# Attention and two expert layers on one core: a narrow key layout for seven pairs of heads, and a fourth tile for the parts of the weights

## The chip, the cores and the metric

The kernel runs on one core of a Trainium2 chip. The metric is the device time in microseconds of one execution, the median of the runs. TensorE (PE, with its weight loads as PEld), VectorE (DVE), ScalarE (ACT) and GpSimd (POOL) are the engines; nearly all transfers are issued from SyncE's queue (SP) and run on the core's 16 DMA engines.

## The reference

Attention over 4 batches of 8 heads, 576 positions of 64 values, with rotary positions on q and k; then a dense layer (512 to 2048 to 512, leaky), then a layer of 8 experts (512 to 1024 to 512) of which each token takes the best one. All in float32.

```python
q_rot, k_rot = rotate(q), rotate(k)
scores = scale * q_rot @ k_rot.T
attn = exp(scores - max); attn = attn / (sum(attn) + 1e-9)
x = (attn @ v)                        # 2304 tokens x 512
h = x @ w_in; x = maximum(0.01 * h, h) @ w_out
out[mask] = gate * relu(x[mask] @ w1[e]) @ w2[e]   # for each expert e
```

## The kernel before

Float32 precision is kept by splitting values into two f16 (or fp32r) parts, a high and a low one, and adding up the products of the parts. Attention works on 16 pairs of heads (g = 0 to 15) and 9 units of each (128 queries of one head; the ninth unit holds the last 64 queries of both heads), 144 units in all.

One pass of `step(i)` (L1006) is written out by hand. It emits the exponential of unit i-1 (L519), the row maximum of unit i (L514), the high and the low part of the weights of unit i-1 into a tile `P` (L525 on ScalarE, L531 on VectorE), its transposition by DMA into `PT` (L535), the product with v of unit i-4 (`LAG` = 4, L552), its evacuation (L562), and the scores of unit i+1 (L507). The order of these letters stands in `ORDER1` (before the dense layer runs), `ORDER2` and `ORDER3`. `P` has 3 buffers, `PT` has 4. Between them, by a budget for each engine, run jobs: the preparation of the next pair, the decoding of the dense layer's weights (`weights`, L201, until about 250 us), and the work on finished rows. After the rows of the first blocks are done, each step also takes one unit of the dense layer: twelve products into `h` (L266), leaky (L274, L278), a split (L282, L286) and six products into `acc` (L297).

`prep(g)` (L372) rotates q and k of a pair, scales them and splits them. The parts go to a staging tile `stg` of four blocks: q's parts of head 0, q's parts of head 1, the high parts of the keys of both heads, and the low ones (`stacks`, L410; `hi`, L417, on ScalarE; `lo`, L423, on VectorE). One DMA transposition makes `kt` from the two key blocks (L472), and in a later piece another makes `stk[:, 0:2]` from the two q blocks (L476). Four copies from `kt` then fill `stk[:, 2:6]` (L479), so that each head has its high keys twice, on partitions 0 to 63 and 64 to 127, and its low keys twice. The scores of a unit are then two products for each half of the keys, with 128 rows each: both parts of q by the high keys, and both parts of q by the low keys. After the copies, the load of the next pair's q and k is issued (L370). `stg` has one buffer, `stk` two.

Of the kernel before, what the change touches and what calls it, by code (L numbers as in the profile page):

```python
# [11 lines left out]
F16 = mybir.dt.float16  # L12
# [9 lines left out]
B, H, S, D = 4, 8, 576, 64  # L22
# [30 lines left out]
NMERGED = 60  # L53
ADDG = 0
HI_A1 = 1
TICK2 = 3
RATE1 = dict(A=2, V=1.8, G=1.4)
RATE2 = dict(A=2, V=2.1, G=1.6)
# [32 lines left out]
def _pow2(nc, pool, sq2, n, inv):  # L91

    t = pool.tile([128, n], U32, name="pt", tag=f"pt{n}")
    s = pool.tile([128, n], F32, name="ps", tag=f"ps{n}")
    nc.vector.tensor_scalar(out=t, in0=sq2.bitcast(U32), scalar1=0xFFFFFFFF, scalar2=24, op0=ALU.bitwise_xor, op1=ALU.logical_shift_right)
    nc.vector.tensor_scalar(out=s.bitcast(U32), in0=t, scalar1=-50.0, scalar2=2.0 ** 23, op0=ALU.add, op1=ALU.mult)
    nc.vector.tensor_scalar(out=inv.bitcast(U32), in0=t, scalar1=-2.0 ** 23, scalar2=304.0 * 2 ** 23, op0=ALU.mult, op1=ALU.add)
    return s
# [3 lines left out]
def attention_moe_kernel(ctx: ExitStack, tc: tile.TileContext, qkv, w_in, w_out, emb, tau, w1, w2,  # L102
                         rope, ident, tokc, iota, pcol, out):
    nc = tc.nc
# [28 lines left out]
    def ps_h():  # L133
        return psH.tile([128, 512], F32, name="h")
# [51 lines left out]
    def decode(raw):  # L186

        hw, lw = raw[:, :, 1], raw[:, :, 0]
        yield Piece(A=1.2, tick=M.tick + (TICK2 if M.unit else TICK))
        nc.scalar.activation(out=hw.bitcast(F32), in_=hw.bitcast(F32), func=AF.Copy, scale=2.0 ** -112)  # L190
# [160 lines left out]
    at = ExitStack()  # L351
    qkp = at.enter_context(tc.tile_pool(name="qkp", bufs=1))
    stp = at.enter_context(tc.tile_pool(name="stp", bufs=2))
    pep = at.enter_context(tc.tile_pool(name="pep", bufs=2))
# [17 lines left out]
    def prep(g):  # L372
        i0 = 9 * (g - 1)
        v16 = v16s[g % 2]
        raw, rawv = raws.pop((g, 2)), raws.pop((g, 1))[:, 0]
        sq = small.tile([128, 3], F32, name="sq3")
        cs, sn = tab[:, 0], tab[:, 1]
        if g:
            t2 = qkp.tile([128, 2, 2, 5, 64], F32, name="t2", tag="stg")
            t2 = [t2[:, t] for t in range(2)]  # L380
        else:
            t2 = [mp.tile([128, 2, 5, 64], F32, name=f"t2{t}", tag="xT", bufs=XTB) for t in range(2)]

        def square(t):
            nc.scalar.activation(out=junk, in_=(raw[:, t] if t < 2 else rawv).rearrange("p h c d -> p (h c d)"), func=AF.Square, accum_out=sq[:, t:t + 1])

        def rope_s(t, eng=nc.gpsimd):
            for z in range(2):
                o, i = 32 * z, 32 - 32 * z
                eng.tensor_tensor(out=t2[t][:, :, :, o:o + 32], in0=raw[:, t, :, :, i:i + 32],  # L390
                                        in1=sn[:, :, o:o + 32].unsqueeze(1).to_broadcast([128, 2, 5, 32]), op=ALU.mult)

        def rope_c(t):
            xf = raw[:, t].rearrange("p h c d -> p h (c d)")
            nc.vector.tensor_tensor(out=xf, in0=xf, in1=cs.rearrange("p c d -> p (c d)").unsqueeze(1).to_broadcast([128, 2, 320]), op=ALU.mult)

        def add(t, eng=nc.vector):
            eng.tensor_tensor(out=raw[:, t], in0=raw[:, t], in1=t2[t], op=ALU.add)

        m3 = small.tile([128, 3], F32, name="m3")  # L400
        sc = small.tile([128, 2], F32, name="sc")

        def scales(pb):
            s3 = _pow2(nc, small, pb[:, 0:3], 3, m3)
            nc.vector.scalar_tensor_tensor(out=sc[:, 0:1], in0=m3[:, 0:1], scalar=0.125, in1=m3[:, 1:2], op0=ALU.mult, op1=ALU.mult)
            nc.vector.tensor_scalar(out=sc[:, 1:2], in0=sc[:, 0:1], scalar1=-1.0, scalar2=None, op0=ALU.mult)
            return s3


        def stacks():  # L410
            stg = qkp.tile([128, 4, 5, 128], F16, name="stg")
            s2 = stg.rearrange("p s c x -> p (s c x)")
            qhi = s2[:, 0:1408].rearrange("p (h x) -> p h x", h=2)[:, :, 0:640].rearrange("p h (c x) -> p h c x", c=5)[:, :, :, 0:64]
            return (s2, qhi, stg[:, 2].rearrange("p c (h x) -> p h c x", h=2), [stg[:, 0, :, 64:128], stg[:, 1, :, 0:64]],
                    [stg[:, 3, :, 64 * h:64 * h + 64] for h in range(2)])

        def hi(out, t):  # L417
            if g and (HIQ, HIK)[t]:
                nc.vector.tensor_scalar(out=out, in0=raw[:, t], scalar1=s3[:, t:t + 1], scalar2=None, op0=ALU.mult)
            else:  # L420
                nc.scalar.activation(out=out, in_=raw[:, t], func=AF.Copy, scale=s3[:, t:t + 1])

        def lo(out, t, high):  # L423
            for h in range(2):
                nc.vector.scalar_tensor_tensor(out=out[h], in0=raw[:, t, h], scalar=s3[:, t:t + 1], in1=high[:, h], op0=ALU.mult, op1=ALU.subtract)

        if g == 0:
            rope_s(1)
            rope_s(0, nc.vector)
            for t in range(3):  # L430
                square(t)
            rope_c(0)
            add(0)
            pb = ps_h()
            nc.tensor.matmul(pb[:, 0:3], lhsT=ones, rhs=sq, start=True, stop=True)
            s3 = scales(pb)
            s2, qhi, khi, qlo, klo = stacks()
            hi(qhi, 0)
            rope_c(1)
            add(1)  # L440
            hi(khi, 1)
            lo(klo, 1, khi)
            lo(qlo, 0, qhi)
        else:
            yield Piece(A=0.72, G=1.64, at=max(i0 - EARLY, 0), tick=M.loaded + TLOAD)
            square(0)
            rope_s(0)
            yield Piece(A=0.72, V=0.74, G=1.64)
            square(1)
            rope_c(0)  # L450
            rope_s(1)
            yield Piece(A=0.72, V=0.74)
            square(2)
            add(0, nc.gpsimd if g < ADDG else nc.vector)
            yield Piece(V=0.74)
            rope_c(1)
            yield Piece(G=1.5)
            add(1, nc.gpsimd)
            pb = yield from total(sq, 3)
            yield Piece(must=True, V=0.35)  # L460
            s3 = scales(pb)
            s2, qhi, khi, qlo, klo = stacks()
            yield Piece(A=1.44)
            hi(qhi, 0)
            hi(khi, 1)
            yield Piece(V=0.93)
            lo(klo, 1, khi)
            yield Piece(V=0.93)
            lo(qlo, 0, qhi)
        yield Piece(at=i0 - 2)  # L470
        kt = stp.tile([128, 2, 640], F16, name="kt", bufs=1)
        nc.sync.dma_start_transpose(out=kt.rearrange("p s (c x) -> p (s c) x", c=5), in_=s2[:, 1280:2560])  # L472
        yield Piece(at=i0 - 1)

        stk = stp.tile([128, 6, 640], F16, name="stk")
        nc.sync.dma_start_transpose(out=stk[:, 0:2].rearrange("p s (c x) -> p (s c) x", c=5), in_=s2[:, 0:1280])  # L476
        for h in range(2):
            for z in range(2):
                nc.sync.dma_start(out=stk[64 * z:64 * z + 64, 2 + 2 * h:4 + 2 * h], in_=kt[64 * h:64 * h + 64])  # L479
        pairs[g] = (stk, s3, sc, v16)  # L480
        if g + 1 < 4 * B:
            load(g + 1, 2)
        vjobs.append(Job(prep_v(g, v16, rawv, s3)))
# [15 lines left out]
    def a_scores(g, u):  # L499
        stk = pairs[g][0]  # L500
        ps = psS.tile([128, 2, 512], F32, name="S")
        todo = [(u % 2, u // 2 * 128, 128, 0)] if u < 8 else [(0, 512, 64, 0), (1, 512, 64, 64)]
        for n in range(2):
            ks = slice(288 * n, 288 * n + 288)
            for h, c0, m, o in todo:
                for a in range(2):
                    nc.tensor.matmul(ps[o:o + m, n, 0:288], lhsT=stk[:, h, c0:c0 + m], rhs=stk[:, 2 + 2 * h + a, ks], start=(a == 0), stop=(a == 1))  # L507
        return ps

    def a_max(g, u, ps):  # L510
# [9 lines left out]
        return e  # L520

    def a_hi(e, i):
        p = pep.tile([128, 2 * S], F16, name="P", bufs=3)
        if i % (HI_ACT if M.unit else HI_A1) == 0:
            nc.scalar.activation(out=p[:, 0:576], in_=e, func=AF.Copy, scale=P_UP)  # L525
        else:
            nc.vector.tensor_scalar(out=p[:, 0:576], in0=e, scalar1=P_UP, scalar2=None, op0=ALU.mult)
        return p
# [440 lines left out]
    n = len(units)  # L969
# [227 lines left out]
    g = gates(0, NCH)  # L1197
# [10 lines left out]
    x = e_xt(3)  # L1208
# [92 lines left out]
```

## Time and profile before

| | us |
|---|---|
| median of 3 runs | 1064.49 |
| lowest and highest | 1061.05, 1064.89 |
| the profiled execution | 1062.26 |
| its span | 1060.5 |
| attention, first to last exponential | 29 to 663 |
| dense layer, first to last product of L266 | 182 to 794 |
| experts | about 800 to 1060 |

All times below are microseconds from the start of the span, in one profiled execution. An engine's busy time leaves out waits; a wait is named by the instruction that waited and by what came last of what it waited for. A row of the timeline gives start, length, engine, line, operation, output and inputs, the count of instructions merged into it, and in brackets the idle time before it with its releaser. The granted clock is 1.00 at TensorE's full 2.4 GHz and 0.50 at 1.2 GHz.

### The profile page before, as it was taken

Reading aid. Unit: us, or ns where it says so; the run is one execution under the profiler, and the core shown is the slowest. Engines: PE = TensorE matmul, PEld = TensorE weight load, DVE = VectorE, ACT = ScalarE, POOL = GpSimd, SP = SyncE. Lnnn points to the kernel's source line nnn. Section 1 sums busy time; section 2 is a strip of 40 time slices with the busy share of each in tenths; the row PEclk is TensorE's granted clock in tenths of the full one; section 3 lists DMA queues with packets and bytes.
Section 4 is the critical chain, followed back from the end, with each engine's and each line's share of the span. In section 5 each row is a group of like instructions: output and inputs, shape, how many; then the busy total and the mean of one; then the engine's idle time right before and its main releaser. Section 6 shows DMA issues by size and latency. Waiting matters only on the chain. (4 is left out here: it accounts for less than half of the span.)

```text
span 1060.5 us, 19876 instructions
## 1 busy us (share of the span) xinstructions
PE 882.0 (83%) x6737; PEld 709.4 (67%) x6737; DVE 773.9 (73%) x1564; ACT 755.8 (71%) x1439; POOL 360.6 (34%) x414
## 2 busy tenths in 40 slices
PE   1455454777888899989898899999999899999997
PEld 1344243565666787767677677778877778888885
DVE  6988798778867874767768766313476999999893
ACT  6987687777767774877777677535345888888883
POOL 1333323252443452544444533322233361211111
PEclk9995555989989999999999999999999999999999
DMA  7899889788487694696795784301152111115190
GB/s 227 192 219 243 194 165 214 171 178 196 91 163 159 120 180 98 122 177 125 140 198 126 125 162 91 66 1 41 31 180 101 40 61 40 51 50 199 34 334 33
DMA packets 269005, 141.41 MB, mean 133 GB/s; under 512 B 236248, under 2 KB 244696, under 8 KB 268897
## 3 DMA queue, kind: packets, MB, share of 16 engines
q1 hardware_dynamic: 265696, 130.11, 54.9%
q0 software_dynamic: 3200, 9.97, 2.9%
q8 instruction: 55, 0.90, 0.4%
q14 instruction: 54, 0.43, 0.1%
HBM read 120.04 MB, written 10.49 MB: 123 GB/s over the span
## 5 line engine op out<-in xcount | busy, mean ns | idle before, releaser
L266 PE MATMUL h<-xT,wi 128*128 128x256 f16 (+1 forms) x1920 | 218.2, 265 | 36.9 <-DVE g L278 31.2
L266 PEld LDWEIGHTS <-wi 128*128 128x128 f16 x1920 | 170.6, 100 | 83.5 <-issue 63.8
L286 POOL TENSOR_TENSOR gl<-g,gh 128x256 fp32r<-128x256 f32 x144 | 110.7, 769 | 317.2 <-ACT gh L282 293.5
L297 PE MATMUL acc<-wo,gh 128*128 128x512 f32 x576 | 196.6, 423 | 0.0
L531 DVE SCALAR_TENSOR_TENSOR P<-E,P 128x576 f16<-128x576 f32 x144 | 127.6, 886 | 92.7 <-ACT P L525 91.8
L552 PE MATMUL o<-v,PT 128*128 128x65 f16 (+3 forms) x1770 | 104.1, 216 | 66.3 <-DMA PT<-P 46.0
L552 PEld LDWEIGHTS <-PT 128*128 128x128 f16 (+1 forms) x1770 | 92.5, 112 | 85.2 <-DMA PT<-P 58.9
L507 PE MATMUL S<-stk 128*128 128x288 f16 (+1 forms) x640 | 115.4, 332 | 36.4 <-ACT E L519 34.5
L278 DVE SCALAR_TENSOR_TENSOR g<-h,uw,g 128x256 f32<-128x256 f32 (+1 forms) x160 | 71.2, 453 | 100.0 <-ACT g L274 99.5
L282 ACT ACTIVATE gh<-g 128x256 fp32r<-128x256 f32 x144 | 59.9, 416 | 94.7 <-DVE g L278 94.1
L525 ACT ACTIVATE P<-E 128x576 f16<-128x576 f32 x144 | 98.2, 682 | 40.1 <-DMA PT<-P 36.5
L519 ACT ACTIVATE E<-S,amx,sc 128x576 f32<-128x576 f32 x144 | 117.9, 818 | 4.9 <-DVE E L514 4.8
L274 ACT ACTIVATE g<-h,uw 128x256 f32<-128x256 f32 (+1 forms) x160 | 69.4, 444 | 72.6 <-PE h L266 68.1
L514 DVE TENSOR_SCALAR_CACHE_REDUCE E<-S,sc 128x576 f32<-128x576 f32 x144 | 116.5, 809 | 0.7 <-PE S L507 0.2
L297 PE MATMUL acc<-wo,gl 128*128 128x512 f32 x288 | 115.6, 401 | 0.0
L297 PEld LDWEIGHTS acc<-wo,gh 128*128 128x128 f32 x576 | 100.9, 193 | 18.6 <-issue 2.5
L507 PEld LDWEIGHTS <-stk 128*128 128x128 f16 (+1 forms) x640 | 58.1, 112 | 54.2 <-issue 39.2
L940 POOL DMA_INDIRECT out<-eo,idi x18 | 25.3, 1405 | 152.8 <-ACT eo L938 142.0
L390 POOL TENSOR_TENSOR t<-raw,tab 128x320 f32<-128x320 f32 x62 | 63.5, 1054 | 13.2 <-DMA raw<-in_qkv 10.1
L297 PEld LDWEIGHTS acc<-wo,gl 128*128 128x128 f32 x288 | 55.2, 192 | 13.7 <-POOL gl L286 0.9
L587 POOL TENSOR_TENSOR x<-xo,rd 128x128 f32<-128x128 f32 (+1 forms) x33 | 20.9, 632 | 102.7 <-DVE rd L579 80.3
L929 PE MATMUL h<-w,hth 128*128 128x512 f32 x176 | 55.4, 396 | 0.4 <-ACT hth L913 0.4
(232 smaller groups left out, 1754.8 us busy)
## 6 DMA issues: line engine op xcount, KB each, us to landing
rb<-in_w SPq DMA_DIRECT2D x78, 512.0 KB
ra<-in_w SPq DMA_DIRECT2D x76, 512.0 KB
stk<-kt SPq DMA_DIRECT2D x64, 160.0 KB
raw<-in_qkv SPq DMA_DIRECT2D x15, 640.0 KB
raw<-in_w_in SPq DMA_DIRECT2D x16, 512.0 KB
raw<-in_w_out SPq DMA_DIRECT2D x16, 512.0 KB
raw<-in_qkv SPq DMA_DIRECT2D x18, 320.0 KB
x2s<-x SPq DMA_DIRECT2D x18, 256.0 KB
```

The lines of the kernel that those rows point to most:

```text
L266: nc.tensor.matmul(m.h[:, c0:c1], lhsT=wi[:, a, c, 128 * f:128 * f + 128], rhs=xT[j][:, 4 * b_ + c, 0:c1 - c0], start=(n == 0), stop=(n == ...
L274: nc.scalar.activation(out=m.g[:, c0:c1], in_=m.h[:, c0:c1], func=AF.Copy, scale=uw[:, f:f + 1])
L278: nc.vector.scalar_tensor_tensor(out=m.g[:, c0:c1], in0=m.h[:, c0:c1], scalar=uw01[:, f:f + 1], in1=m.g[:, c0:c1], op0=ALU.mult, op1=ALU.max)
L286: nc.gpsimd.tensor_tensor(out=m.gl, in0=m.g, in1=m.gh.bitcast(F32), op=ALU.subtract)
L297: nc.tensor.matmul(M.acc[t], lhsT=g_[:, tt], rhs=wo[:, a, f], start=(f == 0 and n == 0), stop=(f == NF - 1 and n == 2))
L390: eng.tensor_tensor(out=t2[t][:, :, :, o:o + 32], in0=raw[:, t, :, :, i:i + 32], in1=sn[:, :, o:o + 32].unsqueeze(1).to_broadcast([128, 2, ...
L507: nc.tensor.matmul(ps[o:o + m, n, 0:288], lhsT=stk[:, h, c0:c0 + m], rhs=stk[:, 2 + 2 * h + a, ks], start=(a == 0), stop=(a == 1))
L514: nc.vector.tensor_scalar(out=e.rearrange("p (a b) -> p a b", a=2), in0=ps[:, :, 0:288], scalar1=pairs[g][2][:, 1:2], scalar2=None, op0=AL ...
L519: nc.scalar.activation(out=e.rearrange("p (a b) -> p a b", a=2), in_=ps[:, :, 0:288], func=AF.Exp, scale=sc[:, 0:1], bias=mx)
L525: nc.scalar.activation(out=p[:, 0:576], in_=e, func=AF.Copy, scale=P_UP)
L531: nc.vector.scalar_tensor_tensor(out=p[:, 576:1152], in0=e, scalar=P_UP, in1=p[:, 0:576], op0=ALU.mult, op1=ALU.subtract)
L552: nc.tensor.matmul(o[ob:ob + m, oc + z:oc + z + w], lhsT=pt[:, i, q0:q0 + m], rhs=v16[:, i, h, c:c + w], start=(n == 0), stop=(n == len(to ...
```

## The change

For pairs 0 to 6 the staging tile is laid out otherwise: blocks 2 and 3 hold the high keys of head 0 and of head 1, each twice side by side, and block 4 holds the low keys of both heads. The second copy of the high keys is written by a VectorE copy. A single transposition of all five blocks then gives `stk[:, 0:5]`; `kt`, its transposition and the four copies fall away, and the piece that waited for them. The first score product of these pairs has 128 rows as before (both parts of q by the high keys); the second takes only the 64 rows of q's high part by the low keys, so the product of the two low parts is left out in these pairs. Pairs 7 to 15 stay as they were, but for the staging tile, which has five blocks for all. The tile `P` gets 4 buffers instead of 3, for all pairs.

```diff
+WIDE = 7
+        wide = g >= WIDE
-            stg = qkp.tile([128, 4, 5, 128], F16, name="stg")
+            stg = qkp.tile([128, 5, 5, 128], F16, name="stg")
-            return (s2, qhi, stg[:, 2].rearrange("p c (h x) -> p h c x", h=2), [stg[:, 0, :, 64:128], stg[:, 1, :, 0:64]],
-                    [stg[:, 3, :, 64 * h:64 * h + 64] for h in range(2)])
+            khi = stg[:, 2].rearrange("p c (h x) -> p h c x", h=2) if wide else stg[:, 2:4, :, 0:64]
+            return (s2, qhi, khi, [stg[:, 0, :, 64:128], stg[:, 1, :, 0:64]],
+                    [stg[:, 3 if wide else 4, :, 64 * h:64 * h + 64] for h in range(2)], stg[:, 2:4, :, 64:128])
...
             hi(khi, 1)
+            lo(qlo, 0, qhi)
+            nc.vector.tensor_copy(out=k2, in_=khi)
             lo(klo, 1, khi)
-            lo(qlo, 0, qhi)
...
+            else:
+                yield Piece(V=1.2)
+                lo(qlo, 0, qhi)
+                nc.vector.tensor_copy(out=k2, in_=khi)
+                yield Piece(V=0.93)
+                lo(klo, 1, khi)
+        if wide:
+            yield Piece(at=i0 - 2)
+            kt = stp.tile([128, 2, 640], F16, name="kt", bufs=1)
+            nc.sync.dma_start_transpose(out=kt.rearrange("p s (c x) -> p (s c) x", c=5), in_=s2[:, 1280:2560])
         yield Piece(at=i0 - 1)
         stk = stp.tile([128, 6, 640], F16, name="stk")
+        if wide:
+            nc.sync.dma_start_transpose(out=stk[:, 0:2].rearrange("p s (c x) -> p (s c) x", c=5), in_=s2[:, 0:1280])
+            for h in range(2):
+                for z in range(2):
+                    nc.sync.dma_start(out=stk[64 * z:64 * z + 64, 2 + 2 * h:4 + 2 * h], in_=kt[64 * h:64 * h + 64])
+        else:
+            nc.sync.dma_start_transpose(out=stk[:, 0:5].rearrange("p s (c x) -> p (s c) x", c=5), in_=s2)
...
+                if g >= WIDE:
+                    for a in range(2):
+                        nc.tensor.matmul(ps[o:o + m, n, 0:288], lhsT=stk[:, h, c0:c0 + m], rhs=stk[:, 2 + 2 * h + a, ks], start=(a == 0), stop=(a == 1))
+                else:
+                    hr = slice(64 * h, 64 * h + 64)
+                    nc.tensor.matmul(ps[o:o + m, n, 0:288], lhsT=stk[:, h, c0:c0 + m], rhs=stk[:, 2 + h, ks], start=True, stop=False)
+                    nc.tensor.matmul(ps[o:o + m, n, 0:288], lhsT=stk[hr, h, c0:c0 + m], rhs=stk[hr, 4, ks], start=False, stop=True)
...
-        p = pep.tile([128, 2 * S], F16, name="P", bufs=3)
+        p = pep.tile([128, 2 * S], F16, name="P", bufs=4)
```

## Rows read from the trace of the kernel before

**Rows 1.** Windows by stage: busy per engine (instructions), granted clock, DMA share, GB/s.

```profile
30.00:182.00 152.00, 75.26 (x707) 53.49 (x705) 133.55 (x303) 119.34 (x235) 47.93 (x48) 0.65 0.90 208
182.00:305.00 123.00, 95.27 (x916) 75.61 (x917) 94.88 (x221) 89.40 (x193) 43.94 (x50) 0.94 0.79 163
305.00:680.00 375.00, 341.37 (x2970) 276.73 (x2970) 259.45 (x615) 268.40 (x587) 163.16 (x220) 0.98 0.70 136
```

**Rows 2.** Waits from 30 to 182 us: total, times, longest.

```profile
DVE P L531 <- ACT P L525: 14.3, 7, 5.4
...
ACT P L525 <- DMA PT<-P: 17.9, 8, 5.8
...
PE o L552 <- DMA PT<-P: 35.6, 13, 8.3
```

**Rows 3.** Windows, columns as above: the stretch from 125 to 130 us.

```profile
125.00:130.00 5.00, 0.00 (x0) 0.00 (x0) 0.53 (x4) 0.00 (x0) 2.48 (x4) 0.50 1.11 288
```

**Rows 4.** Timeline of TensorE and ScalarE at two places; ScalarE's wait, 182 to 680.

```profile
55.93 0.94 PE L552 MATMUL o<-v,PT 128*128 128x65 f16 x14 [4.01 <-DMA PT<-P]
55.97 0.68 ACT L525 ACTIVATE P<-E 128x576 f16<-128x576 f32 x1 [2.53 <-DMA PT<-P]
...
585.70 0.58 PE L552 MATMUL o<-v,PT 128*128 128x129 f16 x9 [0.80 <-DMA PT<-P]
585.74 0.68 ACT L525 ACTIVATE P<-E 128x576 f16<-128x576 f32 x1 [2.17 <-DMA PT<-P]
...
ACT P L525 <- DMA PT<-P: 18.6, 5, 5.2
```

**Rows 5.** Timeline of SP's queue while pair 3 is prepared.

```profile
114.92 1.40 SPq L472 DMA_TRANSPOSE kt<-stg  x1
...
118.68 2.94 SPq L479 DMA_DIRECT2D stk<-kt  x4
...
123.92 1.91 SPq L535 DMA_TRANSPOSE PT<-P  x1
```

**Rows 6.** Windows: one transposition of `P` alone; the copies from `kt`.

```profile
105.00:110.00 5.00, 2.69 (x29) 2.19 (x28) 4.83 (x17) 4.84 (x10) 0.70 (x1) 0.50 0.31 59
...
408.25:410.25 2.00, 2.00 (x14) 1.48 (x13) 0.48 (x1) 0.89 (x2) 0.42 (x1) 1.00 0.89 238
```

**Rows 7.** Timeline of SP's queue and ScalarE while pair 0 is prepared.

```profile
14.12 1.48 SPq L472 DMA_TRANSPOSE kt<-stg  x1
...
17.78 2.45 SPq L479 DMA_DIRECT2D stk<-kt  x4
20.33 0.53 SPq L370 DMA_DIRECT2D raw<-in_qkv  x1
...
26.02 0.74 ACT L385 ACTIVATE junk<-raw 128x640 bf16<-128x640 f32 x1 [3.93 <-DMA raw<-in_qkv]
```

**Rows 8.** Groups by shape on VectorE: busy, mean ns, idle before.

```profile
L395 DVE TENSOR_TENSOR raw<-raw,tab 128x640 f32<-128x640 f32 x32 | 30.5, 954 | 3.9 <-POOL t L390 3.7
...
L764 DVE COPY c<-o 128x256 f32<-128x256 f32 x1 | 0.4, 424 | 0.5 <-PE o L762 0.5
...
L643 DVE COPY enT<-h 128x32 f32<-128x32 f32 x1 | 0.2, 192 | 0.7 <-PE h L641 0.7
```

**Rows 9.** Timeline of TensorE: scores, first dense product, work after scores.

```profile
29.54 1.12 PE L507 MATMUL S<-stk 128*128 128x288 f16 x4 [5.25 <-ACT E L519]
...
182.09 2.72 PE L266 MATMUL h<-xT,wi 128*128 128x256 f16 x12 [2.37 <-DMA xT<-x]
...
293.41 0.65 PE L507 MATMUL S<-stk 128*128 128x288 f16 x4
293.81 0.71 PE L297 MATMUL acc<-wo,gh 128*128 128x512 f32 x2
...
297.06 0.69 PE L507 MATMUL S<-stk 128*64 128x288 f16 x8
297.68 0.50 PE L297 MATMUL acc<-wo,gh 128*128 128x512 f32 x1
```

More of the change, by code (lines that the diff above doesn't have):

```diff
@@ L436, in prep @@
             s3 = scales(pb)
-            s2, qhi, khi, qlo, klo = stacks()
+            s2, qhi, khi, qlo, klo, k2 = stacks()
             hi(qhi, 0)
@@ L461, in prep @@
             s3 = scales(pb)
-            s2, qhi, khi, qlo, klo = stacks()
+            s2, qhi, khi, qlo, klo, k2 = stacks()
             yield Piece(A=1.44)
@@ L465, in prep @@
             hi(khi, 1)
[L466 to L472, printed above, removed]
+            if wide:
+                yield Piece(V=0.93)
+                lo(klo, 1, khi)
+                yield Piece(V=0.93)
+                lo(qlo, 0, qhi)
+            else:
+                yield Piece(V=1.2)
+                lo(qlo, 0, qhi)
+                nc.vector.tensor_copy(out=k2, in_=khi)
+                yield Piece(V=0.93)
+                lo(klo, 1, khi)
+        if wide:
+            yield Piece(at=i0 - 2)
+            kt = stp.tile([128, 2, 640], F16, name="kt", bufs=1)
+            nc.sync.dma_start_transpose(out=kt.rearrange("p s (c x) -> p (s c) x", c=5), in_=s2[:, 1280:2560])
         yield Piece(at=i0 - 1)
         stk = stp.tile([128, 6, 640], F16, name="stk")
[L476 to L479, printed above, removed]
+        if wide:
+            nc.sync.dma_start_transpose(out=stk[:, 0:2].rearrange("p s (c x) -> p (s c) x", c=5), in_=s2[:, 0:1280])
[4 more added lines that the diff above has]
+            nc.sync.dma_start_transpose(out=stk[:, 0:5].rearrange("p s (c x) -> p (s c) x", c=5), in_=s2)
         pairs[g] = (stk, s3, sc, v16)
@@ L505, in a_scores @@
             for h, c0, m, o in todo:
-                for a in range(2):
-                    nc.tensor.matmul(ps[o:o + m, n, 0:288], lhsT=stk[:, h, c0:c0 + m], rhs=stk[:, 2 + 2 * h + a, ks], start=(a == 0), stop=(a == 1))
+                if g >= WIDE:
[5 more added lines that the diff above has]
+                    nc.tensor.matmul(ps[o:o + m, n, 0:288], lhsT=stk[hr, h, c0:c0 + m], rhs=stk[hr, 4, ks], start=False, stop=True)
         return ps
```

## Prediction

> **What bounds the kernel now.** I read the windows by stage first [rows 1]. Two stretches differ. From 30 to 182 us, before the first product of the dense layer at 182.09 [rows 9], VectorE is busy 133.6 of 152 us and the DMA engines 0.90 of the time, while TensorE does 75 us of work. From 182 to 305 TensorE has 95.3 of 123 us, VectorE 94.9, the DMA share is 0.79. From 305 to 680 TensorE has 341 of 375 us and sets the pace alone. The seven changed pairs (g = 0 to 6, units 0 to 62) lie in the first two stretches.
>
> Next the waits of the first stretch [rows 2]. VectorE's 18.4 us without work are mostly one wait: 14.3 us behind ScalarE's high part of the weights (L525). ScalarE waits there 17.9 us, in 8 places, for a transposition of an earlier `P`; TensorE waits 35.6 us in 13 places for the same kind of transposition before the product with v (L552). So VectorE sets the pace, and what stops it are transpositions that land late. From 125 to 130 us one sees it bare: TensorE and ScalarE do nothing, VectorE 0.53 us, DMA is above a full share at 288 GB/s [rows 3]. The transpositions are late because they stand in SP's queue and in the DMA engines behind the burst of a pair's preparation.
>
> The timeline shows what four buffers for `P` meet [rows 4]: the step of unit i writes the `P` of unit i-1 into the buffer of unit i-4, and multiplies `PT` of unit i-4. One landing releases both. In all 13 places ScalarE starts 0.04 us after TensorE, from 55.93/55.97 to 585.70/585.74.
>
> **The change part by part.** The base is the profiled execution's 1062.26 us (span 1060.5 and 1.8 around it); the median of the runs, 1064.49, is 2.2 above it, and I add that at the end.
>
> *Layout, DMA side.* A pair now issues two transpositions of 10 blocks of 128 columns and four copies of 160 KB. SP is held 1.40 us for one transposition and 2.94 for the copies [rows 5], some 5.7 us together; one transposition of 25 blocks is worked out at 25/10 x 1.40 = 3.5. A `PT` waiting behind, as that at 123.92, may be issued 2.2 us earlier. The loads of the next pair's q and k, of v and of the raw weights stand in the same queue and move up by as much. On the DMA engines: a stretch with one `PT` alone (9 blocks) has a share of 0.31 over 5 us, 0.172 us a block [rows 6]. So 20 blocks are 3.4 us, 25 are 4.3. The copies, 655 KB at 238 GB/s and a share of 0.89, take 2.75 x 0.89 = 2.45 us of all engines. Net 3.4 + 2.45 - 4.3 = 1.6 us less per pair, and four pairs (1 to 4) are prepared between 30 and 182: 6.4 us. At worst nothing of it counts (the loads of 512 and 640 KB stay, and they are larger). At best VectorE's whole 14.3 us behind ScalarE go. I take 5, since each burst ends in a stretch like [rows 3] in which only DMA works: **-5** (0 to -14).
>
> *Start.* Pair 0 transposes at 14.12, and its copies can't issue before `kt` has landed, at 17.78; the next pair's load follows at 20.33, and ScalarE stands idle 3.93 us for it until 26.02, ahead of the first exponential [rows 7]. With the one transposition, which now waits for the copy on VectorE too (issue at 14.1 + 0.4), SP is free at 18.0 and the load goes 2.3 us earlier: **-2** (0 to -2.3).
>
> *Four buffers for P.* At each of the 13 places the high part no longer waits, but TensorE's product does, and behind it in TensorE's queue the next unit's scores, for which VectorE's next maximum waits. What is won is at most that ScalarE's high part, 0.68 us [rows 4], and its low part on VectorE lie inside the wait. I take 0.5 a place: 8 places before 182, **-4**, and 5 after, **-2.5**. Ends: 0 (TensorE's product is the next wait and leaves all as it is) and ScalarE's whole 17.9 + 18.6 us. For the first stretch this and the DMA term together are bounded by VectorE's 18.4.
>
> *Added copy.* Each narrow pair adds a VectorE copy of 128x640 f16 (the doubled high keys). No such row stands before. From below a copy of 32 columns, 0.19; from above a two-operand step of 128x640 f32, 0.95; I take the copy of 128x256, 0.42 [rows 8]. Pairs 1 to 4 pay in full, since VectorE sets the pace there, 1.7; pairs 5 and 6 half, 0.4: **+2.1** (0.9 to 5.7). ScalarE's high part keeps its 640 elements. That the keys' transposition now waits for q's low part as well costs nothing: by the code a pair's preparation begins two units before the pair ahead of it does, so its keys have some nine units to land.
>
> *Scores.* The count of products stays, four per unit; every second one has 64 rows. Columns set the time, so I cost the product itself at nothing. What could cost is going from 128 rows to 64 and back. The nearest row is the unit made of two 64-column halves [rows 9]: its eight products take 0.69 us against 0.65 for four whole ones, 0.006 a change; but the next TensorE work starts 0.62 us after its first product against 0.40, 0.22 more for one change in and one out, 0.11 each. Four changes a unit and 27 units (36 to 62) in the stretch where TensorE counts: 0.6 to 11.9 us. I take the inner changes, the nearer case: **+1**. Before 182 TensorE is half idle and covers it.
>
> The Trainium skill has a rule that speaks against this edit: "TensorEngine Tiling (Array Packing)", Key Properties under Tiling Modes, says that changing the tiling mode, not just the tile, drains TensorE. [rows 9] shows 0.11 us at a change between whole and half columns, which agrees with it, and almost nothing between halves; whether rows behave so no row here shows. By that rule the term would be the 11.9, not the 1.
>
> Sum: -5 - 2 - 4 - 2.5 + 2.1 + 1 = -10.4. 1062.26 - 10.4 = 1051.9; with the 2.2, **1054**. Everything after 305 runs the same instructions behind this, so what is won before stays won.
>
> **The rivals.** *Nothing gained.* The loads, not the copies, make the transpositions late, and TensorE's own wait takes the place of ScalarE's. For it: the product waits 35.6 us, twice what ScalarE does. Against: at 125 to 130 the DMA engines are the only ones at work, and 1.6 us of theirs are gone per pair. Half the DMA term, the start, no P term: -2.5 - 2 + 2.1 + 1 = -1.4, so 1063.
>
> *Every change between 128 and 64 rows empties TensorE.* 11.9 instead of 1: 1054 + 10.9 = 1065. It decides from 182 on, where TensorE has 0.77 of the time. The page named above has this as its rule; the traces so far bear it half out.
>
> *Slower: TensorE's clock in the stretch 182 to 305.* The granted clock there is 0.94 on the mean, so some 15 us at the lower level, 1.2 GHz; before 182 the products ran at the lower level all along (four scores 1.12 at 29.54, 0.65 at 293.41 [rows 9]; the clock's record does not name that level before 75 us, the durations do). If halved rows and gaps at the changes leave TensorE at the lower level for half this stretch, 61 us, its 47 us of work there become 47 x 1.12/0.65 = 82; less the 14 us in which it idles now, 20 us more: 1074. Each us at the lower level costs 0.77 x 1.72 - 1 = 0.33, so the gain of 10.4 is lost from 32 us on top of today's 15. Against it: the dense layer's products, most of the work there, keep 128 rows.
>
> **How the numbers follow.** Forecast 0.62, nothing gained 0.18, every change empties 0.08, clock 0.12. A measurement of this kernel tells 0.5% from no change, 5.3 us: faster is below 1059.2, slower above 1069.8. The forecast's own range, from its terms, is 1045 to 1060 and leaves 0.03 to "same": faster 0.59, same 0.29, slower 0.12. The range reaches to the two middle cases and leaves out the clock and the far end of the P term: 1044 to 1067.
>
> **What the changed profile would show.** The first dense product near 171 us, not 182.09 (start 2, DMA 5, P 4, less the copy). No row of ScalarE's L525 waiting for `PT`; TensorE's waits for `PT` from 30 to the first dense product down from 35.6 to some 25, VectorE's gap behind L525 below 7. No copies `stk<-kt` before pair 7, and one transposition of about 3.5 us on SP in their place. A new VectorE copy of 0.2 to 0.95 us, seven times. Scores still near 0.65 us for four after the clock has risen. I am wrong if the first dense product stays within 3 us of 182 (nothing gained), if TensorE's waits move rather than shrink, or if the granted clock between the first dense product and the end of pair 6 falls below about 0.8 (slower).

## The result, and the profile after

The changed kernel takes 1048.16 us (median of 4 runs, 1045.82 to 1052.01) against 1064.41 us of the kernel before in the same set of runs: 0.9858 of the time, 95% interval 0.9821 to 0.9894, 16 us less. The profiled execution takes 1047.53 us, its span 1045.8, 14.7 us less than before.

Windows of the changed kernel by stage, with the columns of [rows 1]:

```profile
30.00:170.00 140.00, 96.77 (x706) 52.26 (x705) 132.21 (x302) 117.49 (x230) 53.32 (x47) 1.00 0.96 209
...
182.00:305.00 123.00, 108.60 (x916) 78.35 (x915) 96.29 (x218) 91.05 (x195) 48.41 (x56) 0.96 0.76 149
305.00:680.00 375.00, 343.14 (x3002) 279.23 (x3000) 250.61 (x606) 265.20 (x582) 157.72 (x217) 0.99 0.70 134
```

In the first stretch VectorE is now busy 132.2 of 140 us; it was 133.6 of 152 [rows 1]. The same work lies closer together. The granted clock of 1.00 in this row isn't what it seems; the last section takes it up. TensorE is busy 96.8 us there and was 75.3 before; the section on the 64 rows shows with what. The waits of the stretch 30 to 170 us of the changed kernel, against [rows 2]: TensorE's for a late transposition, the second row, are less than half, and neither ScalarE's high part (now L547) for a transposition nor VectorE's low part behind it has a row any more.

```profile
PE S L528 <- ACT E L541: 16.0, 18, 2.3
PE o L574 <- DMA PT<-P: 15.2, 8, 4.9
PE o L574 <- ACT xo L584: 12.5, 12, 2.6
```

The start, from the timelines of SP, ScalarE and TensorE, against [rows 7] and the first dense product in [rows 9]:

```profile
14.08 3.92 SPq L496 DMA_TRANSPOSE stk<-stg  x1
18.11 0.50 SPq L371 DMA_DIRECT2D raw<-in_qkv  x1
...
23.77 0.74 ACT L386 ACTIVATE junk<-raw 128x640 bf16<-128x640 f32 x1 [2.65 <-DMA raw<-in_qkv]
...
174.34 2.71 PE L267 MATMUL h<-xT,wi 128*128 128x256 f16 x12 [4.22 <-DMA xT<-x]
```

Where the time went is best seen by the exponential (L519 before) of a pair's first unit. The table has its start in the kernel before, and for each kernel how much earlier (-) or later it starts, each read from one profiled execution; the last column is the last exponential. What follows the last exponential takes 398 us in every one of these kernels.

| unit | 0 | 9 | 27 | 36 | 63 | 90 | 126 | 143 |
|---|---|---|---|---|---|---|---|---|
| before, us | 28.7 | 60.9 | 137.1 | 177.7 | 309.9 | 447.9 | 600.3 | 662.6 |
| changed | -2.3 | -0.8 | -7.0 | -9.9 | -9.5 | -10.4 | -14.9 | -14.8 |
| changed, once more (e8) | -2.9 | -1.5 | -7.7 | -10.3 | -10.1 | -11.4 | -11.9 | -11.9 |
| four P alone (e1) | +0.3 | -0.1 | -2.2 | -1.7 | -2.7 | -2.8 | -7.2 | -7.2 |
| narrow, three P (e2) | -2.2 | -0.7 | -5.9 | -7.9 | -7.0 | -9.7 | -10.0 | -9.1 |
| rows 128 (e3) | -1.8 | -0.3 | -6.6 | -8.9 | -11.2 | -14.6 | -15.3 | -14.4 |
| four narrow pairs (e4) | -2.8 | -1.4 | -7.6 | -7.6 | -10.3 | -11.2 | -13.8 | -13.8 |
| grouped (e5) | -1.7 | -0.2 | -6.5 | -9.4 | -11.8 | -13.8 | -12.2 | -12.2 |
| copies back (e6) | -0.1 | +1.3 | -2.2 | -1.7 | +4.8 | +1.8 | +0.3 | +0.3 |
| thin copies (e12) | -0.3 | +1.2 | -2.1 | -2.3 | +1.2 | -0.8 | -0.2 | -0.2 |
| all narrow (e10) | -2.3 | -0.8 | -7.0 | -10.0 | -10.4 | -9.8 | -9.5 | -1.5 |
| all six blocks (e11) | -1.5 | 0.0 | -5.5 | -9.1 | -12.0 | -16.2 | -20.0 | -18.4 |
| six blocks, 7 pairs (e9) | -1.5 | 0.0 | -5.6 | -9.5 | -7.3 | -9.6 | -13.6 | -12.7 |
| five P (e7) | -2.4 | -0.9 | -7.1 | -9.7 | -8.3 | -14.2 | -17.6 | -16.7 |

The two profiles of the changed kernel differ by 3 us in the last columns, so late differences of that size say nothing. Nor is the middle sharp: e9 and e11 differ only from the preparation of pair 7 on, at about unit 52; they are 2.6 us apart by then, and 4.7 at unit 63. The gain has two places: 10 us before unit 36, and 0.5 (e8) to 4.4 us after unit 90.

### The profile page after: what moved, and what is told of

Read it like the earlier page. It is cut to its first block, busy times and chain, and to the rows that moved or that the text cites. A ratio compares the mean times of both kernels' runs of the same rounds, so it can differ in the third digit from the quotient of the medians.

```text
span 1045.8 us, 19828 instructions
## 1 busy us (share of the span) xinstructions
PE 914.0 (87%) x6737; PEld 706.5 (68%) x6737; DVE 773.3 (74%) x1571; ACT 756.4 (72%) x1439; POOL 364.9 (35%) x414
## 5 line engine op out<-in xcount | busy, mean ns | idle before, releaser
L553 DVE SCALAR_TENSOR_TENSOR P<-E,P 128x576 f16<-128x576 f32 x144 | 124.3, 863 | 61.9 <-ACT P L547 61.6
L547 ACT ACTIVATE P<-E 128x576 f16<-128x576 f32 x144 | 98.3, 682 | 4.1
L528 PE MATMUL S<-stk 128*128 128x288 f16 (+1 forms) x140 | 52.5, 375 | 25.1 <-ACT E L541 24.3
L298 PEld LDWEIGHTS acc<-wo,gl 128*128 128x128 f32 x288 | 55.1, 191 | 13.6 <-POOL gl L287 0.9
L525 PE MATMUL S<-stk 128*128 128x288 f16 (+1 forms) x360 | 53.6, 288 | 5.9 <-ACT E L541 5.6
L609 POOL TENSOR_TENSOR x<-xo,rd 128x128 f32<-128x128 f32 (+1 forms) x33 | 23.4, 708 | 96.9 <-DVE rd L601 58.4
```

Of the source, the lines that this page charges most:

```text
L298: nc.tensor.matmul(M.acc[t], lhsT=g_[:, tt], rhs=wo[:, a, f], start=(f == 0 and n == 0), stop=(f == NF - 1 and n == 2))
L553: nc.vector.scalar_tensor_tensor(out=p[:, 576:1152], in0=e, scalar=P_UP, in1=p[:, 0:576], op0=ALU.mult, op1=ALU.subtract)
```

## The experiments

The theory: the narrow layout relieves the burst at a pair's preparation, before the dense layer starts; four tiles `P` take ScalarE out of the wait for late transpositions. The rivals: each of the two alone is all of it; TensorE's wait takes the place of ScalarE's; the burst is the loads, not the copies.

### Each half alone

**Four tiles alone (e1).** In the kernel before:

```diff
-        p = pep.tile([128, 2 * S], F16, name="P", bufs=3)
+        p = pep.tile([128, 2 * S], F16, name="P", bufs=4)
```

> The kernel before with four tiles P and nothing else; the key layout stays wide for all pairs. My theory: the high part of the weights no longer stands behind a late transposition, some 0.5 us at each of 13 places, so 1058 us (1055 to 1061), with no wait of L525 for PT and TensorE's waits for PT before the first dense product still near 35 us. Rival (TensorE's own wait takes the place of ScalarE's): 1064, no change. Second rival (four tiles are most of the change): 1050.

Measured: 1054.44 us, 0.9904 of before (0.9882 to 0.9926). The gain is 10 us, more than I expected (1055 to 1061) and less than the second rival. But it lies elsewhere than I put it. Up to unit 36 only 1.7 us are won. ScalarE waits for `PT` no more, but TensorE's waits stay (14 places, 37.7 us from 30 to 175): there the rival was right. The rest comes late, in steps of 1 to 2 us at three of the five late stalls. One of them, before (first fence) and with four tiles (second), from the timelines:

```profile
469.21 0.58 PE L552 MATMUL o<-v,PT 128*128 128x129 f16 x9 [2.12 <-DMA PT<-P]
469.25 0.68 ACT L525 ACTIVATE P<-E 128x576 f16<-128x576 f32 x1 [4.20 <-DMA PT<-P]
...
469.84 0.46 ACT L274 ACTIVATE g<-h,uw 128x256 f32<-128x256 f32 x1
...
470.64 0.48 DVE L278 SCALAR_TENSOR_TENSOR g<-h,uw,g 128x256 f32<-128x256 f32 x1
...
471.17 1.18 PE L266 MATMUL h<-xT,wi 128*128 128x256 f16 x6 [0.89 <-DVE g L278]
```

```profile
462.28 0.68 ACT L525 ACTIVATE P<-E 128x576 f16<-128x576 f32 x1
...
464.40 0.47 ACT L274 ACTIVATE g<-h,uw 128x256 f32<-128x256 f32 x1 [1.43 <-PE h L266]
464.90 0.48 DVE L278 SCALAR_TENSOR_TENSOR g<-h,uw,g 128x256 f32<-128x256 f32 x1 [0.95 <-ACT g L274]
...
466.59 0.58 PE L552 MATMUL o<-v,PT 128*128 128x129 f16 x9 [2.29 <-DMA PT<-P]
467.00 0.65 PE L507 MATMUL S<-stk 128*128 128x288 f16 x4
...
467.49 1.47 PE L266 MATMUL h<-xT,wi 128*128 128x256 f16 x12
```

TensorE waits 2.1 and 2.3 us for its transposition, the same. Before, the dense layer's evacuation (L274, then L278) stood behind the waiting L525 on ScalarE, and TensorE's next dense products waited 0.89 us more for it: they start 1.96 us after the release. With four tiles both are done inside the wait, and the dense products start 0.90 us after it. The other two steps aren't the same case over again. At the stall that ends at 507.21, L606, work on finished rows, stands directly behind L525, ahead of L274; TensorE's own wait there falls as well, from 2.25 us to 1.06 with four tiles (502.29). At the one that ends at 585.70, TensorE waits only 0.80, and the next unit's maximum on VectorE starts 1.82 us after the release, behind the low part and L278; with four tiles it starts 1.11 after. What the three have in common is that work behind the waiting L525 gets done inside the wait.

**The narrow layout alone (e2).** The changed kernel with `bufs=3`.

> The changed kernel with three tiles P: the narrow layout alone. My theory: start and DMA relief before the first dense product are its share, so 1055 us (1052 to 1058), unit 36 some 7 us earlier than before, and waits of L547 for PT are back, fewer than the 17.9 us of before in the first stretch. Rival (the loads, not the copies, make the transpositions late): 1062, unit 36 within 3 us of before.

Measured: 1053.72 us, 0.9912 (0.9892 to 0.9932). Unit 36 comes 7.9 us earlier; L547 waits 6.7 us in 3 places for `PT` between 30 and 175 us. As the theory has it. Up to unit 36 the two halves add up (1.7 and 7.9 against 9.9). In all they don't: 0.9904 x 0.9912 would be 0.982, and both together give 0.986. Fewer late transpositions leave less for the fourth tile, but the late columns of the table are not sharp enough to show that.

### What of the narrow layout it is

**The copies put back (e6).** Behind the one transposition of a narrow pair, four copies of the old size to a place that nothing reads:

```diff
             nc.sync.dma_start_transpose(out=stk[:, 0:5].rearrange("p s (c x) -> p (s c) x", c=5), in_=s2)
+            dump = [stp.tile([128, 2, 640], F16, name=nm, bufs=1) for nm in ("kt", "dump")]
+            for h in range(2):
+                for z in range(2):
+                    nc.sync.dma_start(out=dump[h][64 * z:64 * z + 64], in_=s2[64 * h:64 * h + 64, 1280:2560].rearrange("p (s x) -> p s x", s=2))
```

> The changed kernel with four copies of 160 KB from the staging tile to a dump that nothing reads, for the narrow pairs, behind the one transposition: the DMA work and SP's 2.9 us of the removed copies are back, and nothing else. My theory (that work, 2.45 us of all DMA engines a pair, is what was saved before the first dense product): the gain of narrow goes, about 1.5 us a pair for four pairs and 1 to 2 at the start, so 1055 us (1052 to 1058), with TensorE's waits for PT from 30 to 174 us up from 15 to over 25. Rival (the copies are hidden behind the loads, the gain lies elsewhere): 1048, waits as in the changed kernel.

Measured: 1062.21 us, 0.9976 (0.9959 to 0.9993). Up to unit 36 what is left is what four tiles alone give (-1.7 both): the copies are all of the layout's gain there, start included. TensorE's waits for `PT` from 30 to 175 are 24.3 us. Beside the dense layer the copies seem to cost as well: from unit 36 to 63 this kernel loses 6.5 us, the changed one 0.4. The total is worse than I expected, by 7 us.

**The same copies, one fortieth of the bytes (e12).** This puts the step itself to the test: is it the DMA engines' work or SP's queue?

```diff
-... dma_start(out=dump[h][64 * z:64 * z + 64], in_=s2[64 * h:64 * h + 64, 1280:2560].rearrange("p (s x) -> p s x", s=2))
+... dma_start(out=dump[h][64 * z:64 * z + 64, :, 0:16], in_=s2[64 * h:64 * h + 64, 1280:2560].rearrange("p (s x) -> p s x", s=2)[:, :, 0:16])
```

> The kernel with the copies put back, but each copy moves 16 of the 640 columns of a block: SP issues and holds the queue as long as there (four issues, some 3 us a pair), the bytes are one fortieth. My theory (the work of the DMA engines was the cost): near the changed kernel, 1050 (1047 to 1053), unit 36 at most 4 us later than in the changed kernel. Rival (SP's queue, behind which the transpositions and loads stand, was the cost): near the kernel with the full copies, 1062 (1057 to 1064), unit 36 some 8 us later than in the changed kernel.

Measured: 1060.37 us, 0.9969 (0.9948 to 0.9989). My theory falls. Windows of 30 to 170 us, first with the full copies, then with the thin ones:

```profile
30.00:170.00 140.00, 90.58 (x667) 48.88 (x666) 125.30 (x285) 111.86 (x218) 51.52 (x46) 1.00 0.97 219
```

```profile
30.00:170.00 140.00, 91.17 (x669) 49.03 (x668) 126.61 (x286) 112.55 (x218) 51.36 (x46) 1.00 0.91 202
```

The DMA share falls from 0.97 to 0.91 and next to nothing is won: VectorE has done 5.6 us less than in the changed kernel (132.2) with the thin copies, 6.9 with the full ones. What is the same is SP's queue. Its timeline while pair 1 is prepared, in the changed kernel and with the thin copies:

```profile
41.30 3.88 SPq L496 DMA_TRANSPOSE stk<-stg  x1
45.27 0.53 SPq L371 DMA_DIRECT2D raw<-in_qkv  x1
45.90 3.20 SPq L557 DMA_TRANSPOSE PT<-P  x1
```

```profile
43.21 3.86 SPq L496 DMA_TRANSPOSE stk<-stg  x1
47.12 1.31 SPq L500 DMA_DIRECT2D kt<-stg  x2
48.48 1.97 SPq L500 DMA_DIRECT2D dump<-stg  x2
50.55 0.54 SPq L371 DMA_DIRECT2D raw<-in_qkv  x1
51.20 1.44 SPq L561 DMA_TRANSPOSE PT<-P  x1
```

From the end of the pair's transposition to the issue of the next `PT` it is 0.7 us without copies and 4.1 with them, however thin. So it is that four more transfers stand in the queue, 3.4 us of SP's time a pair. Whether SP's time as such counts, or also what each transfer costs the DMA engines apart from its bytes, these runs don't tell apart. SP's time alone doesn't give the sizes: a pair's transpositions and copies hold it some 5.7 us in the wide layout [rows 5], 7.1 with the thin copies and 3.9 in the changed kernel, yet at unit 36 the wide layout with four tiles stands at -1.7, the thin copies at -2.3 and the changed kernel at -9.9.

The Trainium skill, in "DMA: Bandwidth & Descriptors", under "Issuing engines are not separate DMA queues", calls the sequencer's time to start a DMA usually small beside the DMA itself. Here the issues held SP for 3.3 us a pair with nearly no bytes behind them (1.31 and 1.97 above), and the kernel took as long as with all of the bytes.

### What the 64 rows cost

**128 rows in both products (e3).** The low keys of the other head then meet the low part of q, so this kernel doesn't compute the scores; it serves for its time.

```diff
-... lhsT=stk[hr, h, c0:c0 + m], rhs=stk[hr, 4, ks], start=False, stop=True)
+... lhsT=stk[:, h, c0:c0 + m], rhs=stk[:, 4, ks], start=False, stop=True)
```

> The changed kernel with 128 rows in the second score product of the seven narrow pairs too (its result is wrong there: low keys of the other head meet the low part of q). No change between 128 and 64 rows is left; all else is the same. In the trace of the changed kernel the narrow products start 0.226 us apart at the full clock and 0.352 at the lower level. My theory: without the change of rows they start 0.163 and 0.28 apart or less, as the wide ones of before, 0.25 us a unit in the 27 units beside the dense layer, so 1044 us (1041 to 1046). Rival (TensorE waits for others in these units anyway, the changes are covered): 1048, as the changed kernel. Second rival (the spacing comes from the layout, not from the rows): 1048 and the spacing stays.

Measured: 1044.69 us, 0.9819 (0.9797 to 0.9842); the interval just overlaps that of the changed kernel. TensorE's timeline of one unit beside the dense layer, the changed kernel and this one:

```profile
263.35 0.28 PE L528 MATMUL S<-stk 128*128 128x288 f16 x1
263.56 0.29 PE L529 MATMUL S<-stk 64*128 64x288 f16 x1
263.79 0.30 PE L528 MATMUL S<-stk 128*128 128x288 f16 x1
264.02 0.29 PE L529 MATMUL S<-stk 64*128 64x288 f16 x1
264.24 0.73 PE L298 MATMUL acc<-wo,gh 128*128 128x512 f32 x2
```

```profile
262.60 0.28 PE L528 MATMUL S<-stk 128*128 128x288 f16 x1
262.72 0.29 PE L529 MATMUL S<-stk 128*128 128x288 f16 x1
262.84 0.29 PE L528 MATMUL S<-stk 128*128 128x288 f16 x1
262.96 0.29 PE L529 MATMUL S<-stk 128*128 128x288 f16 x1
262.99 0.71 PE L298 MATMUL acc<-wo,gh 128*128 128x512 f32 x2
```

A product takes as long by itself, but it starts 0.21 to 0.23 us after its neighbour where the rows change, and 0.12 where they don't (not 0.163, as I had divided it): about 0.1 us a change. The fourth change of the unit, to the dense layer's product, is dearer: that starts 0.22 us after the last score product, and 0.03 without the change. From a unit's first score product to the next other work it is 0.89 us against 0.39, so the four changes cost 0.50 a unit.

For the 27 units from 36 to 62 that would be 13.5 us. Windows from the exponential of unit 36 to that of unit 63, the kernel before and the changed one:

```profile
177.70:309.90 132.20, 101.01 (x951) 79.58 (x951) 102.17 (x233) 97.76 (x212) 50.71 (x57) 0.91 0.79 162
```

```profile
167.80:300.40 132.60, 114.03 (x968) 81.04 (x966) 103.61 (x239) 97.32 (x210) 48.58 (x56) 0.96 0.78 154
```

TensorE is busy 13.0 us more, and the stretch is 0.4 us longer: its idle time fell from 31.2 us to 18.6. The changes are paid for out of idle time. From unit 36 to 63 the kernel with 128 rows gains 2.3 us on before, and the changed one loses 0.4; but e9, which has 128 rows there too, loses 2.2, so single profiles don't show that the rows make this difference. Before unit 36 there is nothing in it, though TensorE's busy time from 30 to 170 us falls from 96.8 to 73.8: it has idle time to spare there.

**Both whole products first, then both halved ones (e5).**

```diff
-        for n in range(2):
-            for h, c0, m, o in todo:
-                matmul(..., lhsT=stk[:, h, ...], rhs=stk[:, 2 + h, ks], ...)
-                matmul(..., lhsT=stk[hr, h, ...], rhs=stk[hr, 4, ks], ...)
+        for n in range(2):
+            for h, c0, m, o in todo:
+                matmul(..., lhsT=stk[:, h, ...], rhs=stk[:, 2 + h, ks], ...)
+        for n in range(2):
+            for h, c0, m, o in todo:
+                matmul(..., lhsT=stk[hr, h, ...], rhs=stk[hr, 4, ks], ...)
```

> The changed kernel with the four score products of a narrow unit in another order: both of 128 rows, then both of 64, so two changes a unit in place of four. My theory (each change costs some 0.065 us at the full clock and it counts only beside the dense layer): the products that follow one of their own kind start 0.16 apart at the full clock, the unit is 0.13 us shorter, 27 units, 3 us at most: 1046 (1044 to 1048). Rival (what costs is every 64-row product, whatever stands before it): spacing 0.226 throughout and 1048.

Measured: 1046.71 us, 0.9849 (0.9828 to 0.987), beside 1049.35 (0.9868, 0.9842 to 0.9893) for the unaltered changed kernel in the same set (e8). The totals can't be told apart. The timeline can:

```profile
262.78 0.41 PE L530 MATMUL S<-stk 128*128 128x288 f16 x2
263.12 0.41 PE L535 MATMUL S<-stk 64*128 64x288 f16 x2
```

Two products of a kind take 0.41 together, 0.12 more than one; two halved ones do too, and the second pair starts 0.34 us after the first, 0.12 and 0.22. So it is the change that costs, not the 64 rows.

> The changed kernel once more, unaltered, beside the three that follow, so that they can be compared with it on the same chip. Both theories: 1048 us.

**Both parts of the keys doubled (e9).** Six blocks in the staging tile, one transposition of 30 blocks, a second VectorE copy, 128 rows in both products, pairs 0 to 6:

```diff
+            nc.vector.tensor_copy(out=k2[2], in_=k2[1])
...
-            nc.sync.dma_start_transpose(out=stk[:, 0:5].rearrange("p s (c x) -> p (s c) x", c=5), in_=s2)
+            nc.sync.dma_start_transpose(out=stk.rearrange("p s (c x) -> p (s c) x", c=5), in_=s2)
...
```

> The changed kernel with the low keys doubled too, by a second VectorE copy of 0.3 us: one transposition of 30 blocks instead of 25 and no copies by DMA, and both score products with 128 rows, as in the wide layout, for pairs 0 to 6. My theory (the copies by DMA were the cost, the rows of the product another): the DMA gain stays but for 5 blocks, 0.9 us of all DMA engines a pair, four pairs before the dense layer, and TensorE gains the 0.25 us a unit: 1046 (1043 to 1049). Rival (half rows themselves help): 1052 or more.

Measured: 1047.4 us, 0.9854 (0.9828 to 0.9879), the same as the changed kernel. Seven pairs are too few to see the rows in the total.

**All 16 pairs, narrow (e10) and with six blocks (e11).** `WIDE = 16` in the changed kernel and in e9.

> The changed kernel with all 16 pairs narrow, so the product of the two low parts is left out everywhere. My theory: beside the dense layer TensorE sets the pace, and nine more pairs of 9 units at 0.25 us for the changes of rows cost up to 20 us less what the copies gave; after unit 63 the attention loses against the changed kernel: 1054 (1048 to 1062). Rival (copies count everywhere, 2 us a pair): 1040 or less.

> All 16 pairs with both parts of the keys doubled on VectorE, one transposition of 30 blocks, and 128 rows in both products (the kernel with six blocks, for all pairs): no copies by DMA anywhere and no change of rows. My theory: what the changes of rows cost is the distance to the kernel with all pairs narrow, 81 and more units at 0.25 us where TensorE is short, so some 8 us under it, 1044 (1040 to 1050). Rival (rows cost nothing that counts): the same as all narrow within 3 us.

Measured: 1060.62 us (0.9978, 0.9966 to 0.999) against 1045.26 us (0.9827, 0.981 to 0.9845). 15.4 us lie between them, twice the 8 that I expected, and the rows are the chief difference: neither has copies by DMA, and the second has the longer transposition and one VectorE copy more. Windows from the exponential of unit 63 to the last one, all narrow first:

```profile
299.50:661.00 361.50, 355.77 (x2796) 259.85 (x2795) 248.46 (x598) 256.54 (x554) 149.87 (x203) 1.00 0.67 125
```

```profile
297.90:644.20 346.30, 318.66 (x2814) 259.84 (x2813) 254.15 (x607) 255.27 (x556) 151.36 (x204) 0.99 0.72 133
```

With all pairs narrow TensorE is busy 0.98 of this stretch, 37 us more than without changes of rows for as much work, near the 40 that 81 units at 0.50 make. Its idle time takes up 22 of them (27.6 falls to 5.7), and 15 are paid. The kernel with six blocks throughout is the fastest median after e3, which doesn't compute the scores; its interval and that of the changed kernel beside the experiments (e8) overlap by a hair.

**Four narrow pairs (e4).** `WIDE = 4`.

> The changed kernel with four narrow pairs in place of seven: pairs 4 to 6, whose units run beside the dense layer, are wide again. My theory: narrow pays before the dense layer starts, and from unit 36 on the removed copies and the changes of rows cancel (the changed kernel gains nothing between units 36 and 63), so within 3 us of the changed kernel: 1050 (1047 to 1053). Rival (every narrow pair pays its 2 us): 1055, with units 45 to 63 losing 5 us against the changed kernel.

Measured: 1049.76 us, 0.9886 (0.9862 to 0.991), as the theory has it. With pair 4, wide again and prepared before the dense layer starts, 2.3 us are lost at unit 36; at unit 63 the kernel is no longer behind. Within what these profiles resolve, the narrow layout gives and takes the same beside the dense layer.

**Five tiles (e7).** `bufs=5`.

> The changed kernel with five tiles P. My theory: with four the high part waits for no transposition any more (no such row in the changed kernel's trace), so a fifth gives nothing: 1048 (1046 to 1050). Rival (the buffers still set when a transposition may start): 1044 or less.

Measured: 1045.79 us, 0.9862 (0.9832 to 0.9891): nothing beyond the changed kernel.

## Why the prediction was right, point by point

The forecast was 1054, 10.4 us off the profiled time; it became 1048, and 14.7 off the profiled time. The sign and both places (the first stretch, the fourth tile) held; the DMA term had the wrong cause, and the terms of the tiles and of the scores the wrong size. In part the total is luck: the tiles' term is too large before the dense layer and too small after it, and the +1 for the scores stands for a price of 13 us that idle time covers.

*What bounds the kernel.* Right. VectorE set the pace of the first stretch and late transpositions stopped it. The first dense product came at 174.34, not 171; it waited 4.2 us for the transposition of its own input, against 2.4 before [rows 9], which is part of the difference. Unit 36 came 9.9 us earlier, where start, DMA, P and copies had been put at 2 + 5 + 4 - 1.7 = 9.3.

*Layout, DMA side (-5).* Size short, cause wrong. I named SP's 2.2 us a pair and then worked the term out from the DMA engines' 1.6 us a pair. On top of four tiles the layout gives 8.2 us at unit 36 (-1.7 to -9.9); the thin copies take 7.6 of them back with nearly all the bytes gone. The DMA share even rose with the gain, 0.90 to 0.96. The step that failed is reading a share of 0.90 as the bound. What counted was that the four transfers stand in the queue, not their bytes; through what, SP's time or a cost of each transfer on the DMA engines, stays open. Narrow alone with start and copy measures -7.9 at unit 36, so by estimate the term is -6.9 to -8.4 (-7.9 without a start of -2.3 to -0.8 and without the +1.3 of four VectorE copies); the transposition of 25 blocks holds SP 3.9 us (median of seven), not 3.5.

*Start (-2).* -2.3 at unit 0, of which 0.8 are left at unit 9. Every narrow kernel of the table loses 1.3 to 1.5 us between these two units and the one with four tiles alone 0.4; what takes it was not followed.

*Four tiles (-4 and -2.5).* The step "TensorE's product is the next wait" was named as the lower end, and before the dense layer it is nearly that: 1.7 alone, 2.0 on top of narrow, where I took 4. After it I took 0.5 a place for the next unit's maximum, and missed that other work of ScalarE stands behind L525: the dense layer's L274, 1.1 us at the place shown, and the work on finished rows at another. The three steps are 1.0, 2.0 and 1.3 us; from unit 36 to 143 it is 5.5 in sum alone, more than twice my term, and 3.7 on top of narrow, in single profiles.

*Added copy (+2.1).* 0.32 us each, 2.2 of VectorE's time in all seven pairs, against 0.42 each taken.

```profile
L480 DVE COPY stg<-stg 128x640 f16<-128x640 f16 x6 | 1.9, 315 | 0.0
L448 DVE COPY stg<-stg 128x640 f16<-128x640 f16 x1 | 0.3, 327 | 0.0
```

*Scores (+1).* The step was wrong: I took the 0.006 of a change between column halves. A change of rows costs 0.1 us and more, like the 0.11 that [rows 9] had for a change between whole and half columns. That was the rival "every change empties TensorE", and the rule of the Trainium skill behind it ("TensorEngine Tiling (Array Packing)", Key Properties) agrees with what these runs show: 0.50 us a unit, 13.5 over 27 units. The sign "scores still near 0.65 for four" failed with it: the four narrow products at 263.35 take 0.96 from the first start to the last end. The rival's time was still wrong, because TensorE had 31 us of idle time from unit 36 to 63 that covers the 13. With nine more narrow pairs, where less is idle, 15 of 37 us are paid.

*Nothing gained; TensorE's clock.* Neither came. TensorE's waits for `PT` fell from 35.6 to 15.2 us, and the granted clock between 182 and 305 is 0.96, not below 0.94.

## What to carry to other kernels

Where transfers of several kinds go through one issuing queue, count the transfers ahead of the critical one and SP's time for each, not only bytes and the share of the DMA engines: try fewer transfers, even if the one that is left is longer. A fourth buffer whose wait ends with another engine's wait for the same transfer isn't useless; look for what else stands behind the waiting instruction on its own engine. Put products with the same row count next to each other, and look at TensorE's idle time in the stretch: up to that much, the changes are covered.

## What the runs showed of the hardware

Four transfers of 64 partitions a pair cost the same whether each moved 160 KB or a fortieth of it (1062.2 and 1060.4 us, 0.9976 and 0.9969 of the kernel before). A change between score products of 128 and 64 rows costs TensorE about 0.1 us at the full clock, one to the dense layer's product 0.19; products of either kind in a row cost nothing extra. The record of the granted clock can't be taken at its word before its first change: the two profiles of the changed kernel show 1.00 and 0.50 from 106 to 109 us, with the same four score products, the second to fourth 0.33 to 0.36 us after the one before; at 263.35 us, at the full clock, it was 0.21 to 0.23.

```profile
106.00:109.00 3.00, 2.29 (x19) 1.14 (x18) 2.93 (x10) 2.97 (x6) 0.00 (x0) 1.00 1.16 217
```

```profile
106.00:109.00 3.00, 1.74 (x11) 0.58 (x9) 2.90 (x11) 2.97 (x7) 0.24 (x1) 0.50 1.19 210
```

The first is the profile of the change, the second that of e8. So the clock of the whole span, 0.991 against 0.935 before, is no gain of this change: the fastest of its four runs (1045.82 us) has 0.939.
